# Three-part follow-up of a first product, and the order of two products around the masks, in an attention and mixture-of-experts kernel

## The chip, the cores and the metric

The kernel runs on one core of a Trainium2 chip. The metric is the device time of one execution in microseconds (us). The engines are PE (TensorE: matmuls; its weight loads are PEld), DVE (VectorE), ACT (ScalarE), POOL (GpSimd) and SP (SyncE, which only issues DMAs here). Each engine works through its own instructions in order; an instruction that waits holds back all that stands behind it on its engine.

## What is computed

Three networks follow each other: attention in which only scores within tau of the row's maximum count, a dense two-layer network with an ELU, and a layer of eight experts of which each token takes one.

```python
def _attn_ref(q, k, v, tau):                       # 2 batches, 8 heads, 576 tokens, 64 wide
    scores = scale * np.matmul(q, k.transpose(0, 1, 3, 2))
    thresh = np.max(scores, axis=-1, keepdims=True) - tau
    scores = np.where(scores >= thresh, scores, -1000000000.0)
    ...
    return np.matmul(attn, v)
def _moe_ref(x, w_in, w_out):                      # 1152 tokens, 512 -> 2048 -> 512
    h = x @ w_in
    g = np.where(h > 0.0, h, alpha * (np.exp(np.minimum(h, 0.0)) - 1.0))
    return g @ w_out
def _moe2_ref(x, w_gate, w1, w2, capacity):        # 8 experts, 512 -> 1024 -> 512
    expert_idx = np.argmax(x @ w_gate, axis=1)
    ...
    h = np.maximum(np.einsum('ecd,edf->ecf', disp, w1), 0.0)
    y = np.einsum('ecf,efd->ecd', h, w2)
```

## The kernel before

Matmuls run in float16 on numbers split in a high and a low half, with three products for one (high by high, high by low, low by high), so nearly every tile is followed by a copy of its high half (ACT) and a subtraction for its low half (POOL or DVE).

The 1152 tokens are nine tiles of 128. The first 38 passes of the program are **steps** (the loop over `i`, written out under a manual schedule, so that the order of the code is the order on every engine). Step `i` treats one pair of heads of one tile (four steps to a tile) and carries along pieces of the later networks:

- `emit_pv(i - 2)`: the product of the probabilities of two steps ago (`pt`) with the values (`vst`), into `pv`.
- `emit_max`: DVE takes the maxima of the two score tiles `s` (L267), and from them `nb` (L268) and `th` (L269). `emit_exp`: ACT's exponentials (L273) into `pp`. `emit_mask`: DVE's masks (L279), which also read `s`. A score tile has two buffers, so the scores of the next step (`emit_s`, L245) wait for the mask: those of the next step's first head stand behind the first mask, those of the second head are written at the end of the step.
- `emit_split` and `emit_pt`: ACT and POOL (L288, L289) split `pp` into `phl`, and a transposing DMA brings it into `pt` (L294).
- `conv_next`: in steps 0 to 16, the conversion of one of 32 chunks of the dense network's weights (three DVE, two ACT, one POOL instruction each).
- `emit_x`: after a tile's last pair, its attention output is normalized and transposed into `xt`.
- `piece()`: one **first product** (`mm1_chunk`, L386: 48 matmuls into the bank `mma`) or one **second product** (`mm2_chunk`, L416: 12 matmuls into the bank `mmb`) of the dense network, taken in turn where both are ready. A table, `FILL`, says how many a step gets: one ahead of the masks, the rest behind them. What follows a first product (`after`: ACT's `ef` L400 and L401, DVE's `gf` L402, ACT's `g` L405, POOL's `g` L406) is written by `flush`, at the end of the step or just ahead of the step's next first product, which needs the bank `mma` back.
- `settle` and `slot`, at the end of the step: when a tile's second products are complete, `route` writes the token rows `x` (`x2_hi` L440, `x2_lo` L445; two row buffers), transposes them (`x2t`), and over the next steps computes the logits (L513), chooses the expert and counts (`choose`), ranks and scatters the rows to memory (`place`, `dispatch`, an indirect DMA of POOL's queue, L494). Each call of `slot` moves every open route on to its next `yield`.
- `prep_k`, `prep_v`, `prep_q`: keys, values and queries are split ahead of use; the low half of a tile's queries is POOL's (L105, once in four steps).

After the steps a **tail** finishes the dense network (a while loop of single pieces, now ordered by the scheduler, and the last tile by `last_block`), and then the **experts** run (L664, L720) while their weights stream in (`stg`, `we`, L624, L627).

## Time and profile before

| what | value |
|---|---|
| time, median of 3 runs | 705.2 us (705.11 to 707.5) |
| time of the profiled execution | 703.61 us |
| its span, first to last instruction | 701.8 us |
| PE busy | 477.0 us (68%) |
| DVE, ACT, POOL busy | 387.8 (55%), 357.6 (51%), 267.7 us (38%) |
| mean granted clock of TensorE | 0.895 of full speed |

The profiled execution is 1.8 us longer than its span (what lies around the instructions) and 1.6 us shorter than the median. Busy shares are means over stages of different kinds; the rows below take them stage by stage. Times in rows are us from the start of the span.

### The profile page before, as it was taken

Reading aid. Unit: us, or ns where it says so; the run is one execution under the profiler, and the core shown is the slowest. Engines: PE = TensorE matmul, PEld = TensorE weight load, DVE = VectorE, ACT = ScalarE, POOL = GpSimd, SP = SyncE. Lnnn points to the kernel's source line nnn. Section 1 sums busy time; section 2 is a strip of 40 time slices with the busy share of each in tenths; the row PEclk is TensorE's granted clock in tenths of the full one; section 3 lists DMA queues with packets and bytes.
Section 4 is the critical chain, followed back from the end, with each engine's and each line's share of the span. In section 5 each row is a group of like instructions: output and inputs, shape, how many; then the busy total and the mean of one; then the engine's idle time right before and its main releaser. Section 6 shows DMA issues by size and latency. Waiting matters only on the chain. (4 is left out here: it accounts for less than half of the span.)

```text
span 701.8 us, 12999 instructions
## 1 busy us (share of the span) xinstructions
PE 477.0 (68%) x5343; PEld 382.2 (54%) x5343; DVE 387.8 (55%) x768; ACT 357.6 (51%) x511; POOL 267.7 (38%) x193
## 2 busy tenths in 40 slices
PE   1133455558455677587776778789778999887793
PEld 0022244346235445455554547556678999876781
DVE  1778895944962644453445543543862556664731
ACT  1455474654553544444355544444663776565641
POOL 1244563543451323234344433432233334153332
PEclk9999998878667799988899989999899999999897
DMA  6447576672764551822428453255764889888631
GB/s 217 118 126 191 156 189 186 140 187 39 175 163 121 140 128 35 222 65 50 113 54 226 87 94 59 58 98 152 263 230 98 248 239 253 259 247 255 201 88 48
DMA packets 150771, 105.59 MB, mean 150 GB/s; under 512 B 135209, under 2 KB 135209, under 8 KB 146608
## 3 DMA queue, kind: packets, MB, share of 16 engines
q1 hardware_dynamic: 148064, 99.94, 54.9%
q0 software_dynamic: 2640, 4.74, 1.9%
q8 instruction: 44, 0.72, 0.4%
q14 instruction: 23, 0.19, 0.1%
HBM read 60.06 MB, written 12.68 MB: 104 GB/s over the span
## 5 line engine op out<-in xcount | busy, mean ns | idle before, releaser
L386 PE MATMUL mma<-xt,wi 128*128 128x128 f16 x1728 | 119.1, 237 | 24.4 <-DVE gf L402 19.8
L386 PEld LDWEIGHTS <-wi 128*128 128x128 f16 x1728 | 115.4, 108 | 29.0 <-issue 21.6
L245 PE MATMUL s<-kst,qst 128*128 128x288 f16 (+1 forms) x320 | 58.4, 344 | 104.2 <-DVE pp L279 95.2
L289 POOL TENSOR_TENSOR phl<-pp,phl 128x1152 f16<-128x1152 f32 x36 | 85.3, 2370 | 102.9 <-issue 95.5
L416 PE MATMUL mmb<-wo,g 128*128 128x512 f16 x384 | 107.0, 439 | 17.5 <-DVE x L445 14.6
L402 DVE SCALAR_TENSOR_TENSOR gf<-ef,mma 128x512 f32<-128x512 f32 x36 | 24.7, 687 | 143.4 <-ACT ef L401 143.4
L245 PEld LDWEIGHTS <-qst 128*128 128x128 f16 (+1 forms) x320 | 30.1, 115 | 124.4 <-DVE pp L279 73.2
L627 DVE SCALAR_TENSOR_TENSOR we<-stg,we 128x1024 f16<-128x1024 f32 x64 | 79.0, 1268 | 32.3 <-ACT we L624 30.7
L273 ACT ACTIVATE pp<-s,nb,escale 128x576 f32<-128x576 f32 x72 | 55.9, 827 | 77.6 <-DVE nb L268 77.6
L624 ACT ACTIVATE we<-stg 128x1024 f16<-128x1024 f32 x64 | 64.3, 1048 | 43.6 <-DMA stg<-in_w_dram 42.8
L406 POOL TENSOR_TENSOR g<-gf,g 128x512 f16<-128x512 f32 x36 | 42.4, 1179 | 106.3 <-ACT g L405 106.2
L664 PE MATMUL mm<-xs,we 128*128 128x196 f16 x768 | 72.4, 259 | 14.8 <-DVE yt L731 5.2
L416 PEld LDWEIGHTS <-g 128*128 128x128 f16 x384 | 40.9, 111 | 71.2 <-issue 43.6
L664 PEld LDWEIGHTS <-we 128*128 128x128 f16 x768 | 69.1, 103 | 16.9 <-DVE we L627 9.1
L311 PE MATMUL pv<-vst,pt 128*128 128x64 f16 (+3 forms) x1080 | 52.9, 216 | 30.1 <-ACT vst L107 11.4
L311 PEld LDWEIGHTS <-pt 128*128 128x128 f16 (+1 forms) x1080 | 49.7, 114 | 37.3 <-issue 34.8
L677 POOL TENSOR_TENSOR ht<-rf,ht 128x392 f16<-128x392 f32 x32 | 35.6, 1123 | 77.7 <-issue 39.1
L279 DVE SCALAR_TENSOR_TENSOR pp<-s,th,pp 128x576 f32<-128x576 f32 x72 | 55.9, 814 | 15.2 <-ACT pp L273 15.2
L720 PE MATMUL mm<-ht,we 128*128 128x196 f16 x672 | 57.9, 247 | 1.7 <-DVE yt L731 1.7
L720 PEld LDWEIGHTS <-we 128*128 128x128 f16 x672 | 56.9, 97 | 1.8 <-issue 1.8
L400 ACT ACTIVATE ef<-mma 128x512 f32<-128x512 f32 x36 | 21.5, 596 | 71.3 <-PE mma L386 71.2
L288 ACT ACTIVATE phl<-pp 128x1152 f16<-128x1152 f32 x36 | 42.0, 1165 | 24.6 <-DVE pp L279 24.6
(123 smaller groups left out, 608.4 us busy)
## 6 DMA issues: line engine op xcount, KB each, us to landing
stg<-in_w_dram SPq DMA_DIRECT2D x32, 1024.0 KB, 6.1
cst<-in_w_in_dram SPq DMA_DIRECT2D x16, 512.0 KB, 4.5
cst<-in_w_out_dram SPq DMA_DIRECT2D x16, 512.0 KB, 4.0
disp<-zero SPq DMA_DIRECT2D x6, 771.0 KB, 4.7
qraw<-in_qt_dram SPq DMA_DIRECT2D x9, 512.0 KB, 3.4
vraw<-in_vb_dram SPq DMA_DIRECT2D x8, 320.0 KB, 5.9
kraw<-in_kt_dram SPq DMA_DIRECT2D x8, 288.0 KB
out_dram<-zero SPq DMA_DIRECT2D x1, 2304.0 KB
```

Of the source, the lines that this page charges most:

```text
L245: nc.tensor.matmul(s[a:z, half, 0:288], q2[:, pas, h, a:z], kst[b, h // 2][:, h % 2, half * 288:(half + 1) * 288], start=(pas == 0), stop= ...
L273: nc.scalar.activation(out=pp[:, z].rearrange("p (a c) -> p a c", a=2), in_=s, func=ACTF.Exp, bias=nb[:, z:z + 1], scale=escale,)
L279: nc.vector.scalar_tensor_tensor(out=e, in0=s, scalar=th[:, z:z + 1], in1=e, op0=ALU.is_ge, op1=ALU.mult, accum_out=rsum[t_][:, h:h + 1],)
L289: nc.gpsimd.tensor_tensor(out=d[:, 1], in0=flat, in1=d[:, 0], op=ALU.subtract)
L311: nc.tensor.matmul(o[a:e, h:h + w // D, :].rearrange("p h d -> p (h d)"), q[:, ph * 9 + blk, a:e], vt[:, vh, c:c + w], start=(blk == 4 and ...
L386: nc.tensor.matmul(ps[:, o * P:(o + 1) * P], w[:, wh, kk, :], xt[t_][:, xh * 4 + kk, :], start=(k_ == 0), stop=(k_ == 11),)
L406: nc.gpsimd.tensor_tensor(out=lo, in0=g, in1=hi, op=ALU.subtract)
L416: nc.tensor.matmul(ps, gt[t_, q][:, gh, o, :], w[:, wh, :], start=(first and o == 0 and n == 0), stop=(last_ and o == QF - 1 and n == 2),)
L624: nc.scalar.activation(out=w[:, 0, part], in_=t[:, part], func=ACTF.Copy, scale=SC)
L627: nc.vector.scalar_tensor_tensor(out=w[:, 1, part], in0=t[:, part], scalar=SC, in1=w[:, 0, part], op0=ALU.mult, op1=ALU.subtract)
L664: nc.tensor.matmul(ps[:, o * n:(o + 1) * n], w[:, wh, kk % 2, f * P:(f + 1) * P], t[:, xh * 4 + kk, :], start=(k_ == 0), stop=(k_ == 11),)
L720: nc.tensor.matmul(ps[:, o * n:(o + 1) * n], w[:, wh, f % 4, j * P:(j + 1) * P], h2[:, gh, f, :], start=(f == 0 and n_ == 0), stop=(f == 7 ...
```

## The change

Four things change. The generator `after` now yields twice, so that its five instructions come in three parts: ACT's two for `ef`; DVE's `gf`; the two halves of `g`. `flush(1)` moves every open one on by one part, and in a step it stands at three places: ahead of the maxima, behind the exponentials, and behind the first conversion, so a first product's follow-up goes into the **next** step. The pieces are ordered: ahead of the masks only second products (`piece(2)`; a first one only in a step with conversions, none open and no second product ready), and one first product, if one is ready, at the end of the step, just ahead of the second head's scores (`piece(1)`). `settle` and `slot` move ahead of that last piece. The matmuls of `choose` that count tokens become `count`, one `yield` later, so a route takes one slot more. `FILL` starts a step earlier.

```diff
-    FILL = [0] * 8 + [3] * 11 + [2] * (NTILE * NPAIR + LAG - 19)
+    FILL = [0] * 7 + [3] * 11 + [2] * (NTILE * NPAIR + LAG - 18)
...
             nc.scalar.activation(out=e, in_=e, func=ACTF.Exp, scale=-1.0, bias=lnsc)
+            yield
             nc.vector.scalar_tensor_tensor(
                 out=g, in0=e, scalar=-GS, in1=ps, op0=ALU.add, op1=ALU.max
             )
+            yield
             nc.scalar.activation(out=hi, in_=g, func=ACTF.Copy)
             nc.gpsimd.tensor_tensor(out=lo, in0=g, in1=hi, op=ALU.subtract)
-        return after
+        return after()
...
-        rk, oh, pr, slot_f = choose(rp)
+        oh, pr, slot_f = choose(rp)
+        yield
+        rk = count(rp[:, 64:64 + E], oh)
         yield
...
-    def flush():
-        while evac:
-            evac.pop(0)()
-
-    def piece():
+    def flush(stages=3):
+
+        for _ in range(stages):
+            for g in list(evac):
+                if next(g, g) is g:
+                    evac.remove(g)
+
+    def piece(first=0):
         a, b = pick1(), pick2()
         if a is None and b is None:
             return False
-        if b is None or (a is not None and turn[0] == 0):
+        if first == 2 and b is None:
+            return False
+        if b is None or (a is not None and first < 2):
...
-            g_at[a, q] = step[0]
+            g_at[a, q] = step[0] + 1
...
+            flush(1)
             if on:
                 lim = emit_max([sc[z] for z in range(2)])
                 for z in range(2):
                     emit_exp(sc[z], lim[0], pair_p[i], z)
+            flush(1)
             if nc_:
                 conv_next()
-            if nf:
-                piece()
+            flush(1)
+            for _ in range(nf - 1):
+                piece(2) or (nc_ and not evac and piece(1))
             if on:
...
                 emit_split(i)
                 emit_pt(i)
+            settle()
...
-            for _ in range(nf - 1):
-                piece()
+            slot()
+            if nf:
+                piece(1)
             if i + 1 < NSTEP:
                 sc[1] = emit_s((i + 1) // NPAIR, (2 * i + 3) % H)
-            flush()
-            settle()
...
-            slot()
...
-        piece()
+        piece(1 + step[0] % 2)
```

What the planner makes of it: the steps from 7 to 18 hold 11 first products instead of 12 (two each in steps 7, 11, 12 and 15, one in 16, 17 and 18; before, two in 8, three in 11, one in 12, three in 15, one in 17, two in 18). From step 19 on every step has one second and one first product in both kernels. The tail gets one first product more.

DVE in a step in which a tile's output `xf` is normalized and a route chooses its expert (rows mx to slot_f). Before, from the masks (L279) to the next step's maxima:

```order
L279 SCALAR_TENSOR_TENSOR pp,rsum<-s,th,pp 128x576 x2
L324 TENSOR_SCALAR rinv<-rsum 128x8
L325 RECIPROCAL rinv<-rinv 128x8
L327 TENSOR_TENSOR xf<-pv,rinv 128x512
L402 SCALAR_TENSOR_TENSOR gf<-ef,mma 128x512
L453 TENSOR_REDUCE mx<-mmc 128x1
L454 SCALAR_TENSOR_TENSOR cand<-mmc,mx,ev 128x8
L457 TENSOR_REDUCE amin<-cand 128x1
L459 TENSOR_SCALAR oh<-ev,amin 128x8
L463 TENSOR_SCALAR nmx<-mx 128x1
L467 TENSOR_SCALAR slot_f<-amin 128x1
L267 TENSOR_REDUCE m<-s 128x1 x2
```

Now, the same kind of step from its own maxima on:

```order
L267 TENSOR_REDUCE m<-s 128x1 x2
L268 TENSOR_SCALAR nb<-m,cmul 128x2
L269 TENSOR_SCALAR th<-m,cadd 128x2
L403 SCALAR_TENSOR_TENSOR gf<-ef,mma 128x512
L279 SCALAR_TENSOR_TENSOR pp,rsum<-s,th,pp 128x576 x2
L324 TENSOR_SCALAR rinv<-rsum 128x8
L325 RECIPROCAL rinv<-rinv 128x8
L327 TENSOR_TENSOR xf<-pv,rinv 128x512
L455 TENSOR_REDUCE mx<-mmc 128x1
```

`gf`, which waits for the first product, stood between the masks and the next maxima; now it stands between a step's own maxima and its masks.

ACT in a step that also prepares the queries (qraw, qst) and writes rows (x). Before, from the exponentials (L273) on:

```order
L273 ACTIVATE pp<-s,nb,escale 128x576 x2
L288 ACTIVATE phl<-pp 128x1152
L400 ACTIVATE ef<-mma 128x512
L401 ACTIVATE ef<-ef,lnsc 128x512
L405 ACTIVATE g<-gf 128x512
L103 ACTIVATE qraw<-qraw 128x1024
L104 ACTIVATE qst<-qraw 128x1024
L440 ACTIVATE x_3727<-mmb 128x512
```

Now:

```order
L273 ACTIVATE pp<-s,nb,escale 128x576 x2
L407 ACTIVATE g<-gf 128x512
L288 ACTIVATE phl<-pp 128x1152
L464 ACTIVATE pr<-mmc,nmx 128x8
L442 ACTIVATE x_3584<-mmb 128x512
L103 ACTIVATE qraw<-qraw 128x1024
L104 ACTIVATE qst<-qraw 128x1024
L400 ACTIVATE ef<-mma 128x512
L401 ACTIVATE ef<-ef,lnsc 128x512
L273 ACTIVATE pp<-s,nb,escale 128x576 x2
```

The rows `x` come ahead of the queries, and the two `ef` instructions now stand behind the queries, directly ahead of the next exponentials.

DVE in step 22, where the third tile's rows are written (x_3007; the first tile's rows, x_2159, hold one of the two row buffers). Now, from the scatter's numbers on:

```order
L490 CAST slot_i<-slot_f 128x1
L491 TENSOR_REDUCE den<-pr 128x1
L492 TENSOR_SCALAR den<-den 128x1
L493 RECIPROCAL den<-den 128x1
L495 TENSOR_SCALAR x_2159<-den 128x1
L496 COPY x_2159<-ids 128x1
L497 TENSOR_TENSOR cum<-cum,oh 128x8
L447 SCALAR_TENSOR_TENSOR x_3007<-mmb,x_3007 128x512
L267 TENSOR_REDUCE m<-s 128x1 x2
```

Before, a whole step lay between the first tile's `cum` row and the third tile's rows; now the rows follow in the same step.

## Rows read from the trace of the kernel before

**Rows 1.** Four stretches: busy us of each engine (instructions), granted clock, DMA share, GB/s.

```profile
95.00:275.00 180.00, 107.79 (x1189) 81.86 (x1190) 110.78 (x189) 94.51 (x133) 78.63 (x53) 0.80 0.55 137
275.00:463.00 188.00, 139.82 (x1640) 101.38 (x1638) 86.55 (x249) 87.48 (x117) 72.38 (x44) 0.88 0.45 100
463.00:536.00 73.00, 62.84 (x803) 49.76 (x802) 39.15 (x109) 38.77 (x60) 22.17 (x17) 0.92 0.62 186
536.00:673.00 137.00, 120.58 (x1353) 118.24 (x1352) 78.56 (x98) 85.94 (x131) 51.31 (x41) 0.96 0.80 228
```

**Rows 2.** Line L268, two stretches: count, ns min/median/max, first and last start in us.

```profile
L268 DVE TENSOR_SCALAR nb<-m,cmul x13: 228/297/557, 95.2 to 274.9; 128x2 f32<-128x2 f32 x13
...
L268 DVE TENSOR_SCALAR nb<-m,cmul x17: 228/228/554, 274.9 to 462.9; 128x2 f32<-128x2 f32 x17
```

**Rows 3.** Waits from 275 to 463: who for whom, us in total, times, longest.

```profile
DVE gf L402 <- ACT ef L401: 77.2, 16, 6.7
...
PE mmb L416 <- DVE x L445: 14.6, 4, 4.8
```

**Rows 4.** Timeline, step 28: start, us, engine, line, op, tiles [idle before <-releaser].

```profile
384.01 1.15 POOL L406 TENSOR_TENSOR g<-gf,g 128x512 f16<-128x512 f32 x1 [2.60 <-ACT g L405]
384.64 0.55 DVE L268 TENSOR_SCALAR nb<-m,cmul 128x2 f32<-128x2 f32 x1
...
387.04 0.66 PE L245 MATMUL s<-kst,qst 128*128 128x288 f16 x4 [1.99 <-DVE pp L279]
...
387.54 2.84 PE L386 MATMUL mma<-xt,wi 128*128 128x128 f16 x48
...
390.22 0.65 PE L245 MATMUL s<-kst,qst 128*128 128x288 f16 x4
...
391.01 1.03 PE L311 MATMUL pv<-vst,pt 128*128 128x128 f16 x27
...
391.45 2.68 SPq L294 DMA_TRANSPOSE pt<-phl  x1
...
391.87 0.69 DVE L402 SCALAR_TENSOR_TENSOR gf<-ef,mma 128x512 f32<-128x512 f32 x1 [4.15 <-ACT ef L401]
391.88 2.75 PE L416 MATMUL mmb<-wo,g 128*128 128x512 f16 x12
392.47 1.42 DVE L267 TENSOR_REDUCE m<-s 128x1 f32<-128x576 f32 x2
```

**Rows 5.** Timeline, step 30, with queries and rows; columns as in rows 4.

```profile
408.26 2.38 POOL L289 TENSOR_TENSOR phl<-pp,phl 128x1152 f16<-128x1152 f32 x1 [4.46 <-issue]
...
412.79 0.69 DVE L402 SCALAR_TENSOR_TENSOR gf<-ef,mma 128x512 f32<-128x512 f32 x1 [5.87 <-ACT ef L401]
...
415.12 1.06 ACT L104 ACTIVATE qst<-qraw 128x1024 f16<-128x1024 f32 x1
416.08 0.58 ACT L440 ACTIVATE x<-mmb 128x512 f16<-128x512 f32 x1
416.26 2.13 POOL L105 TENSOR_TENSOR qst<-qraw,qst 128x1024 f16<-128x1024 f32 x1 [0.88 <-ACT qst L104]
...
417.44 4.44 PE L416 MATMUL mmb<-wo,g 128*128 128x512 f16 x12 [4.84 <-DVE x L445]
```

**Rows 6.** Timeline, step 11 (conversions and three first products); columns as in rows 4.

```profile
149.87 5.23 PE L386 MATMUL mma<-xt,wi 128*128 128x128 f16 x48 [5.14 <-DVE gf L402]
...
157.27 4.33 PE L386 MATMUL mma<-xt,wi 128*128 128x128 f16 x48 [2.16 <-DVE gf L402]
...
163.08 0.69 DVE L402 SCALAR_TENSOR_TENSOR gf<-ef,mma 128x512 f32<-128x512 f32 x1 [5.86 <-ACT ef L401]
...
165.13 0.55 DVE L268 TENSOR_SCALAR nb<-m,cmul 128x2 f32<-128x2 f32 x1
```

**Rows 7.** DMA issues: tiles, queue, count, median us from issue to landing.

```profile
pt<-phl SPq DMA_TRANSPOSE x36, 4.6
...
disp<-x,slot_i POOLq DMA_INDIRECT x9, 3.2
```

More of the change, by code (lines that the diff above doesn't have):

```diff
@@ L447, in x2_lo, with choose @@
         )
-    def choose(rp, rk=None):
+    def choose(rp):
         lg = rp[:, 0:E]
@@ L459, in choose @@
         nc.vector.tensor_scalar(oh, ev, amin, None, ALU.is_equal)
-        rk = (rp if rk is None else rk)[:, 64:64 + E]
-        nc.tensor.matmul(rk, ones, cum, start=True, stop=False, skip_group_check=True)
-        nc.tensor.matmul(rk, tri, oh, start=False, stop=True, skip_group_check=True)
         nc.vector.tensor_scalar(nmx, mx, -I2, None, ALU.mult)
@@ L467, in choose, with count @@
         nc.vector.tensor_scalar(slot_f, amin, float(CS), float(E * CS), ALU.mult, ALU.add)
-        return rk, oh, pr, slot_f
+        return oh, pr, slot_f
+    def count(rk, oh):
+        nc.tensor.matmul(rk, ones, cum, start=True, stop=False, skip_group_check=True)
+        nc.tensor.matmul(rk, tri, oh, start=False, stop=True, skip_group_check=True)
+        return rk
     def rank(rk, oh):
@@ L576, in route_last @@
         x2 = row.bitcast(F16)
-        rk, oh, pr, slot_f = choose(rp, mm_bank())
+        oh, pr, slot_f = choose(rp)
+        rk = count(mm_bank()[:, 64:64 + E], oh)
         bank = []
@@ L779 @@
     evac = []
-    turn = [0]
     def ready(kind, q, ahead=0):
@@ L824, in piece @@
             return False
-        if b is None or (a is not None and turn[0] == 0):
+        if first == 2 and b is None:
+            return False
+        if b is None or (a is not None and first < 2):
             q = nq1[a]
             nq1[a] += 1
-            turn[0] = 1
             bank = "a"
@@ L831, in piece @@
             evac.append(mm1_chunk(a, q, bank))
-            g_at[a, q] = step[0]
+            g_at[a, q] = step[0] + 1
             return True
         t_, q1 = b
-        turn[0] = 0
         if not summing:
```

## Prediction

> **What bounds the kernel now.** I read the stretches first, then the waits, then the order of events in single steps. The stretches [rows 1] show four stages. The experts (536 to 673) keep PE busy 120.6 of 137 us; the change does not touch them. The tail (463 to 536) has PE busy 62.8 of 73 us. The two stretches of steps are different: from 95 to 275 no engine is busy much over 60% of 180 us, and from 275 to 463 PE is busy 139.8 of 188 us at a granted clock of 0.88, DVE and ACT less than half. So the steps wait rather than work. The waits [rows 3] name it: DVE stood 77.2 us in 16 steps in front of `gf`, for ACT's `ef`, and PE 14.6 us in four steps in front of a second product, for DVE's `x2_lo`.
>
> One undisturbed step shows the loop [rows 4]. Between `nb` at 384.64 and the end of the next maxima at 393.89, where the next `nb` starts, lie 9.25 us, and each link waits for the one before it: nb to the first head's scores 2.40 (exponential, mask), to the first product 0.50, to the second head's scores 2.68, to `gf` 1.65 (ACT's two `ef` instructions), to the next maxima 0.60, their length 1.42. The scores were written by 390.87, but the maxima start at 392.47, because `gf` stands ahead of them on DVE and waits for the first product's follow-up. The end of step 30 shows what else stands there [rows 5]: from `gf` at 412.79 DVE dispatches rows and waits for ACT's queries and rows, and PE stands 4.84 us until 417.44, then works its second product at the lower clock (4.44 us instead of 2.75). Sixteen steps from step 19 to step 35 take 274.9 to 462.9, 188.0 us or 11.75 each [rows 2].
>
> In the earlier stretch the same follow-up is paid once for every first product that another one follows: in step 11 the second starts at 149.87 and the third at 157.27 [rows 6], 7.40 us apart, each having waited for `gf` of the one before; and behind the third, from `gf` at 163.08 to `nb` at 165.13, 2.05 us, with the two `ef` ahead of it.
>
> **Steps 19 to 34.** What the change removes from the loop is `gf` with its wait, and everything that `settle` and `slot` put between `gf` and the maxima. What is left of the serial chain, from the start of the second head's scores: the scores 0.65, the second maximum 0.71 (half of 1.42), some 0.15 of hand-over, then nb to the first head's scores 2.40: 3.9 us. PE meanwhile has 390.22 to 391.01 (scores, logits in this step), `pv` 0.87 and a second product 2.75: 4.1 us without the logits. So PE is late last, by a little. A step is then PE's own work: scores and first product 0.50 + 2.68, scores 0.49, `pv` 0.87, second product 2.75, together 7.3 us [rows 4], all at full clock, which I take since PE would hardly idle and the experts, with PE busy 88%, are granted 0.96 [rows 1].
>
> The rest is moved, not removed. `ef` runs while the second head's scores and maxima do. `gf` stands between `th` and the masks, where DVE waits for the exponential anyway; if `ef` is late, the masks are late by as much. `hi` of `g` stands ahead of `phl` on ACT, which waits for the second mask; `lo` of `g` (1.15 on POOL) ends about when POOL's `phl` can start. `x2_lo` and `dispatch` run beside PE's first product (2.68) and scores. The probabilities: the transposing DMA was issued 6.81 us after `nb` (391.45) and lands 4.6 later [rows 7], 11.4 in all; `pv` asks for it two steps on, two steps of 7.3 less the 1.5 by which `nb` follows the scores, 13.1 us, plus 0.5. The cover is thin (about 2 us) but holds.
>
> Three costs are added.
>
> First, the queries. In one step of four ACT's two passes and then POOL's 2.13 us [rows 5] now fall on the next step's `nb`. What happens then, rows 4 show: `nb` took 0.55 us at 384.64 where its median is 0.228 [rows 2], and ended at 385.19, with POOL's instruction of 384.01 to 385.16. DVE's small instruction does not finish while POOL's runs. Count from the start of the second head's scores: `nb` follows about 1.5 later (scores, second maximum, hand-over), the probabilities' DMA 6.8 behind that, at 8.3; POOL's 2.38 for `phl` [rows 5] comes before it, so ACT's split ends at about 5.8. Then follow ACT's rows, 0.58, and two passes of 1.06 each, to 8.5, and POOL's queries, to 10.6, while the next `nb` is due at 7.3 + 1.5 = 8.8 and takes 0.23: 1.6 us late, of which PE's margin takes 0.2, so 1.4. A fourth kind of step has `dispatch` run into POOL's `phl` in the same way; I take 0.7. With the logits (0.45), that is 2.6 us in four steps, 0.65 a step. I round 7.95 up to 8.0.
>
> The Trainium skill ("SBUF — State Buffer", section "Who interferes with whom") has this as a lock: of a DVE instruction in a two-port mode and a GpSimd one, whichever starts first holds the shared ports for its whole length and the other blocks fully. The trace agrees in the 0.55 above. It speaks against the change: with the lock a step is 8.0, without it 7.5, and the total 8 us less.
>
> Second, the row buffer. In step 22 the third tile's rows need the buffer that the first tile's scatter, issued in the same step, still reads, since a route now takes a slot more. The scatter stands on POOL behind `phl`, so it starts about 8.3 us after the scores began and lands 3.2 later [rows 7], 11.5; then ACT's rows 0.58, DVE's as long as its `gf`, 0.69, and the next maxima 1.42: 14.2 instead of 8.8, over 5 us, and PE idles meanwhile and comes back at the lower clock, some 1.5 more: 6.5 us, once. For the later tiles the scatter lies at least a step ahead.
>
> Third, 1.5 us for loads and zero fills that now share fewer microseconds with the probabilities.
>
> Sum: 16 x 8.0 + 6.5 + 1.5 = 136 against 188: **-52 us**. Bounds: PE's bare 7.3 a step without any of the small collisions (117 + 6.5, -64 us); and the loop of rows 4 as it is, 9.25, without what `slot` adds to it (148 + 6.5, -33 us). I choose nearer the first, because each link of the shorter chain has its row, and keep both for the range.
>
> **Steps 7 to 18** take 95.2 to 274.9, 179.7 us [rows 2]. Steps 11 and 15 lose a third first product each, 7.40 [rows 6]: -14.8. Six steps ended in a first product (8, 11, 12, 15, 17, 18) and no longer have its follow-up between the scores and the maxima: 6 x 2.15 (the 2.05 of rows 6, and a little for `ef`): -12.9. Step 18 has one first product for two: its 2.84 [rows 4] and a wait for `gf` of about half a microsecond, -3.4. Step 12 gets a second one behind a first: 7.40, less the second product of 2.75 that leaves it: +4.6. The second products that go to steps 13 and 14, and the one first product of step 16, run beside conversions. Sum **-26.5 us**; bounds -18 (step 12 pays in full, and loads of keys and values hold steps 15 to 18) and -34 (PE's clock stays up in those steps; the 4.33 and 5.23 of rows 6 were at the lower one).
>
> **Tail.** One first product more, 2.84 [rows 4], and routes that end a slot later: **+3.5 us**; between 0 (it fills PE's 10 idle us of 73 [rows 1]) and 7.4 (it stands alone with its follow-up, as in rows 6). The steps 0 to 6 and the experts stay.
>
> **Total.** -52 - 26.5 + 3.5 = -75 us. From the profiled execution's own 703.6 us that gives 628.6; the median of the runs is 1.6 us above the profiled one, so against 705.2 it would be 630. I say **628 us**. The ends of the three parts give 606 (-64, -34, 0) and 660 (-33, -18, +7.4).
>
> **Rivals.**
>
> *Another engine closes the loop (0.17).* DVE and ACT have long in-order queues; if `ef` comes late behind the queries, the masks, the scores and PE follow, and a step is 9 to 10 us rather than 8. For it: ACT's 87.5 us in 16 steps is 5.5 a step, with three hand-overs to DVE in each. Against it: nothing on ACT between the masks and the first product's end fills more than 5 us except in the query step. Time: 16 x 1 to 2 us more, 645 to 660.
>
> *Row buffer or probabilities late at every tile (0.07).* If not only step 22 waits for its scatter but each of six later tiles, or `pv` for its DMA as often, at 6.5 us each it is 39 us more: 667. For it: two buffers, a route of six slots, a new tile every four steps, and only about 2 us of cover for `pv`. Against it: after step 22 the scatter comes at least a step before the rows that need its buffer.
>
> *The clock (0.03), the other side.* If denser work on PE brought the granted clock down to its lower level, a step would be 14.6 us instead of 7.3, sixteen of them 234, and the whole 703.6 + 46 - 26.5 + 3.5 = 727 us, slower than before. It decides from a mean clock of about 0.55 in the steps: there, 16 x 7.3 / 0.55 = 212 us eat up both gains. For it: the steps from 95 to 275 had 0.80 [rows 1]. Against it: that stretch had PE busy 60%, the experts with 88% had 0.96, and the slow second product of rows 5 came behind 4.84 us of idling.
>
> *The gain does not come (0.03).* Some order that I misread keeps the old loop, and only the third first products are saved: about 688.
>
> **Numbers.** The forecast's own case, 605 to 645 us, holds 0.70, the rivals 0.17, 0.07, 0.03 and 0.03. For 8 in 10 I take 606 to 656: the forecast's case and most of the first rival. Half a per cent is about what a measurement of this kernel can tell from no change: faster by more 0.95, within it 0.02, slower by more 0.03.
>
> **What would show it.** In the changed kernel's profile the starts of `nb` in steps 19 to 35 should lie 7.3 to 9 us apart, except behind step 22 (about 14). DVE's wait for `ef` should fall from 77 to under 15 us, PE's wait for `x2_lo` should be gone but for step 22, and PE's clock in these steps should be above 0.93. Steps 11 and 15, with two first products each, should take about 16 us. `nb` behind the queries should be long. The forecast is wrong if steps stand at 9 us or more with PE waiting for DVE's masks, if `pv` waits for its DMA, if ACT's rows wait for the scatter at more than one tile, or if the tail grows by over 8 us.

## The result: 634 us, 0.897 of the time before

Timed beside the kernel before on one chip, the changed kernel took 634.18 us (median of 4 runs, 631.46 to 635.73) against 706.35 us (4 runs, 705.11 to 709.11): a ratio of 0.897, 95% interval 0.892 to 0.902. A second set on another occasion gave 632.22 us (6 runs) against 704.73 (11 runs): 0.896, 0.893 to 0.899. The prediction was 628 us, 606 to 656. The profiled execution took 635.48 us, its span is 633.7, and the mean granted clock 0.925 instead of 0.895.

Steps 19 to 34 of the changed kernel (columns as in rows 1):

```profile
253.00:390.00 137.00, 123.37 (x1639) 92.15 (x1638) 101.57 (x238) 85.01 (x117) 72.29 (x44) 0.96 0.68 134
```

PE is busy 123 of 137 us; before, it was busy 140 of 188 [rows 1]. It executes the same matmuls, faster, at a clock of 0.96 instead of 0.88. The starts of `nb` bound the steps (count, shortest, median and longest ns, first and last start):

```profile
L268 DVE TENSOR_SCALAR nb<-m,cmul x12: 228/230/927, 96.2 to 244.1; 128x2 f32<-128x2 f32 x12
...
L268 DVE TENSOR_SCALAR nb<-m,cmul x16: 228/228/2178, 253.2 to 383.5; 128x2 f32<-128x2 f32 x16
```

Steps 7 to 18 take 253.2 - 96.2 = 157 us (179.7 before), and steps 19 to 34, up to the next `nb` at 390.3, 137.1 us (188.0 before) [rows 2], 8.6 each instead of 11.75.

The waits of that stretch, in the form of rows 3. A line for DVE's `gf` waiting for ACT's `ef`, 77.2 us before [rows 3], is not among them any more:

```profile
ACT ef L400 <- PE mma L386: 17.7, 12, 2.7
DVE x L447 <- ACT x L442: 13.4, 4, 6.6
DVE m L267 <- PE s L245: 11.6, 10, 2.5
...
ACT x L442 <- DMA disp<-x,slot_i: 8.5, 1, 8.5
...
PE mmb L418 <- DVE x L447: 6.5, 1, 6.5
...
PE pv L311 <- DMA pt<-phl: 3.0, 2, 2.5
...
PE s L245 <- DVE pp L279: 2.3, 5, 1.1
```

DVE and ACT now wait for PE (the first and third lines). The ten waits of the maxima lie in nine of the 16 steps. In the other seven (19, 20, 22, 28, 29, 31 and 33) the maxima follow other work of DVE without a wait, as in step 28 (timeline):

```profile
337.93 2.37 POOL L289 TENSOR_TENSOR phl<-pp,phl 128x1152 f16<-128x1152 f32 x1 [0.45 <-POOL g L408]
338.31 2.01 DVE L497 TENSOR_TENSOR cum<-cum,oh 128x8 f16<-128x8 f16 x1
...
340.24 1.41 DVE L267 TENSOR_REDUCE m<-s 128x1 f32<-128x576 f32 x2
```

`cum` starts without a wait and lasts until POOL's `phl` ends, and the maxima come right behind it. PE waits once for rows, 6.5 us, behind the one wait for the scatter, and hardly for the masks.

Step 24, undisturbed, from its `nb` to the next (timeline; what is in brackets is idle time before, and who ended it):

```profile
301.89 0.23 DVE L268 TENSOR_SCALAR nb<-m,cmul 128x2 f32<-128x2 f32 x1
...
302.16 0.68 DVE L403 SCALAR_TENSOR_TENSOR gf<-ef,mma 128x512 f32<-128x512 f32 x1
...
304.36 0.65 PE L245 MATMUL s<-kst,qst 128*128 128x288 f16 x4
...
304.90 2.84 PE L386 MATMUL mma<-xt,wi 128*128 128x128 f16 x48
...
307.58 0.65 PE L245 MATMUL s<-kst,qst 128*128 128x288 f16 x4
...
308.27 0.76 DVE L267 TENSOR_REDUCE m<-s 128x1 f32<-128x576 f32 x1 [2.46 <-PE s L245]
...
308.93 2.75 PE L418 MATMUL mmb<-wo,g 128*128 128x512 f16 x12
309.06 0.23 DVE L268 TENSOR_SCALAR nb<-m,cmul 128x2 f32<-128x2 f32 x1
```

From 301.89 to 309.06 are 7.17 us, and no PE instruction in it has an idle time in front. `gf` follows `nb` without a wait, and the second maximum waits 2.46 us for the scores where it used to wait for `gf` [rows 4].

Step 22, the long one:

```profile
277.55 0.65 DVE L268 TENSOR_SCALAR nb<-m,cmul 128x2 f32<-128x2 f32 x1
...
282.05 2.38 POOL L289 TENSOR_TENSOR phl<-pp,phl 128x1152 f16<-128x1152 f32 x1 [0.45 <-POOL g L408]
...
282.43 2.02 DVE L497 TENSOR_TENSOR cum<-cum,oh 128x8 f16<-128x8 f16 x1
...
284.60 1.15 POOL L498 DMA_INDIRECT disp<-x,slot_i  x1 [0.17 <-PE s L245]
...
290.44 0.60 ACT L442 ACTIVATE x<-mmb 128x512 f16<-128x512 f32 x1 [8.52 <-DMA disp<-x,slot_i]
...
291.81 5.00 PE L418 MATMUL mmb<-wo,g 128*128 128x512 f16 x12 [6.45 <-DVE x L447]
...
293.12 2.18 DVE L268 TENSOR_SCALAR nb<-m,cmul 128x2 f32<-128x2 f32 x1
293.16 2.12 POOL L105 TENSOR_TENSOR qst<-qraw,qst 128x1024 f16<-128x1024 f32 x1 [7.41 <-ACT qst L104]
```

ACT's rows wait 8.52 us for the scatter, DVE's rows and the maxima stand behind them, PE idles 6.45 us and returns at the lower clock (5.00 instead of 2.75). The step takes 15.58 us. In the last two lines, and in `cum` beside `phl`, a DVE instruction of a few elements lasts until POOL's ends.

Where the 68.1 us went (us, from the starts of `nb` in the profiled executions; the last two columns are the time of that execution and the median):

| kernel | to step 0 | steps 0-6 | steps 7-18 | steps 19-34 | behind | profiled | median |
|---|---|---|---|---|---|---|---|
| before | 23.1 | 72.1 | 179.7 | 188.0 | 238.9 | 703.61 | 706.35 |
| changed | 24.1 | 72.1 | 157.0 | 137.1 | 243.4 | 635.48 | 634.18 |
| changed, again | 25.0 | 72.1 | 157.6 | 134.8 | 243.3 | 634.86 | 632.22 |
| follow-up whole | 23.2 | 72.1 | 172.9 | 184.7 | 243.7 | 698.18 | 696.68 |
| settle late | 23.7 | 72.1 | 163.6 | 135.0 | 244.9 | 641.22 | 638.29 |
| pieces as before | 24.8 | 72.1 | 162.4 | 138.2 | 235.9 | 635.06 | 636.25 |
| count early | 23.3 | 72.1 | 158.7 | 145.5 | 239.5 | 641.51 | 639.94 |
| queries on DVE | 23.8 | 77.1 | 160.7 | 136.2 | 244.3 | 643.98 | 642.74 |
| three rows | 25.3 | 72.1 | 156.7 | 127.2 | 246.5 | 629.69 | 628.83 |
| short second product | 24.9 | 72.1 | 156.4 | 138.9 | 246.1 | 640.28 | 634.59 |
| zeros in parts | 23.7 | 72.1 | 157.2 | 134.8 | 239.5 | 629.25 | 631.65 |
| rows and zeros | 25.0 | 72.1 | 158.4 | 128.8 | 239.5 | 625.92 | 626.53 |

The column "behind" holds the tail and the experts, up to the end of the span. The first expert matmul parts them, before and now:

```profile
L664 PE MATMUL mm<-xs,we x768: 244/248/373, 535.9 to 672.3; 128*128 128x196 f16 x192
...
L671 PE MATMUL mm<-xs,we x768: 244/248/373, 470.7 to 604.9; 128*128 128x196 f16 x192
```

The tail grew from 73.0 to 80.5 us, and what follows it fell from 165.9 to 162.9.

The two executions of the changed kernel show how far a column can be trusted: 1 us in steps 7 to 18, 2 in steps 19 to 34.

### The profile page after: what moved, and what is told of

It is laid out like the page before. It is cut to its first block, busy times and chain, and to the rows that moved or that the text cites. A ratio compares the mean times of both kernels' runs of the same rounds, so it can differ in the third digit from the quotient of the medians.

```text
span 633.7 us, 13023 instructions
## 1 busy us (share of the span) xinstructions
PE 452.4 (71%) x5343; PEld 367.6 (58%) x5343; DVE 405.0 (64%) x768; ACT 354.4 (56%) x511; POOL 267.8 (42%) x193
## 4 chain that ended last, share of the span: by engine, by line
DVE 38%; DMA 22%; PE 16%; ACT 11%; issue 10%; POOL 2%; SPq 1%; DVEq 0%; POOLq 0%; ACTq 0%
DMA stg<-in_w_dram 8%; PE mma L386 8%; DVE pp L279 7%; DVE m L267 6%; DMA out_dram<-y,ix 5%; DVE cvp L359 4%; DVE we L634 3%; DVE cvp L358 3%; PE mmb L418 3%; DMA pt<-phl 3%; DMA yr<-yt 2%; DVE kst L213 2%; PE s L245 2%; ACT we L631 2%; DVE cvp L362 2%
## 5 line engine op out<-in xcount | busy, mean ns | idle before, releaser
L386 PE MATMUL mma<-xt,wi 128*128 128x128 f16 x1728 | 116.2, 233 | 33.1 <-DVE gf L403 33.1
L386 PEld LDWEIGHTS <-wi 128*128 128x128 f16 x1728 | 111.2, 106 | 37.1 <-issue 25.4
L245 PE MATMUL s<-kst,qst 128*128 128x288 f16 (+1 forms) x320 | 56.2, 333 | 72.5 <-DVE pp L279 63.4
L418 PE MATMUL mmb<-wo,g 128*128 128x512 f16 x384 | 95.8, 403 | 12.1 <-DVE x L447 6.5
L289 POOL TENSOR_TENSOR phl<-pp,phl 128x1152 f16<-128x1152 f32 x36 | 85.3, 2371 | 14.8 <-POOL g L408 9.2
L273 ACT ACTIVATE pp<-s,nb,escale 128x576 f32<-128x576 f32 x72 | 55.9, 827 | 49.2 <-DVE nb L268 49.1
L671 PE MATMUL mm<-xs,we 128*128 128x196 f16 x768 | 69.6, 253 | 14.3 <-DVE g L754 4.8
L671 PEld LDWEIGHTS <-we 128*128 128x128 f16 x768 | 66.7, 100 | 16.2 <-DVE we L634 8.1
L418 PEld LDWEIGHTS <-g 128*128 128x128 f16 x384 | 37.5, 103 | 56.7 <-issue 22.3
L311 PE MATMUL pv<-vst,pt 128*128 128x64 f16 (+3 forms) x1080 | 48.5, 208 | 30.7 <-DVE xf L327 11.9
L267 DVE TENSOR_REDUCE m<-s 128x1 f32<-128x576 f32 x72 | 52.0, 750 | 27.0 <-PE s L245 26.7
L311 PEld LDWEIGHTS <-pt 128*128 128x128 f16 (+1 forms) x1080 | 46.2, 108 | 37.1 <-issue 30.5
L727 PEld LDWEIGHTS <-we 128*128 128x128 f16 x672 | 57.4, 98 | 2.4 <-issue 2.3
L279 DVE SCALAR_TENSOR_TENSOR pp<-s,th,pp 128x576 f32<-128x576 f32 x72 | 55.9, 813 | 4.4 <-ACT pp L273 4.3
L288 ACT ACTIVATE phl<-pp 128x1152 f16<-128x1152 f32 x36 | 41.9, 1165 | 12.7 <-DVE pp L279 12.7
```

Source lines behind the costliest of these rows:

```text
L245: nc.tensor.matmul(s[a:z, half, 0:288], q2[:, pas, h, a:z], kst[b, h // 2][:, h % 2, half * 288:(half + 1) * 288], start=(pas == 0), stop= ...
L267: nc.vector.tensor_reduce(out=m[:, z:z + 1], in_=sc[z], axis=AX.XY, op=ALU.max)
L273: nc.scalar.activation(out=pp[:, z].rearrange("p (a c) -> p a c", a=2), in_=s, func=ACTF.Exp, bias=nb[:, z:z + 1], scale=escale,)
L279: nc.vector.scalar_tensor_tensor(out=e, in0=s, scalar=th[:, z:z + 1], in1=e, op0=ALU.is_ge, op1=ALU.mult, accum_out=rsum[t_][:, h:h + 1],)
L289: nc.gpsimd.tensor_tensor(out=d[:, 1], in0=flat, in1=d[:, 0], op=ALU.subtract)
L311: nc.tensor.matmul(o[a:e, h:h + w // D, :].rearrange("p h d -> p (h d)"), q[:, ph * 9 + blk, a:e], vt[:, vh, c:c + w], start=(blk == 4 and ...
```

## Experiments

**Which part of the change carries the gain.** Three kernels undo one part each.

The follow-up whole again, at the end of the step:

```diff
-            flush(1)
...
-            flush(1)
...
-            flush(1)
...
                 sc[1] = emit_s((i + 1) // NPAIR, (2 * i + 3) % H)
+            flush()
```

> The changed kernel with the follow-up of a first product written whole at the end of the step, as before the change; the order of the pieces, the earlier settle and slot and the later count stay. My theory, that the three parts in the next step take gf out of the way of the maxima and that this is the larger part of the gain: the steps 19 to 34 take 9.2 to 9.7 us each instead of 8.6, and up to 160 us together instead of 137; the steps from 7 to 18 lose some 10 us as well; the time is 660 to 672. DVE's wait for ef comes back (over 40 us in these steps). Rival, that the gain comes from settle and slot, which no longer stand between gf and the maxima: within 5 us of 634.

Measured: 696.68 us, 0.989 of before (0.984 to 0.995). Nearly all of the gain is gone, more than I had expected. Its step 27 (timeline):

```profile
364.93 0.56 DVE L268 TENSOR_SCALAR nb<-m,cmul 128x2 f32<-128x2 f32 x1
...
368.05 0.28 PE L245 MATMUL s<-kst,qst 128*128 128x288 f16 x1 [2.78 <-DVE pp L279]
...
373.28 0.69 DVE L403 SCALAR_TENSOR_TENSOR gf<-ef,mma 128x512 f32<-128x512 f32 x1 [4.63 <-ACT ef L401]
373.88 1.42 DVE L267 TENSOR_REDUCE m<-s 128x1 f32<-128x576 f32 x2
```

The scores of 371.63 are written by 372.28, but the maxima begin at 373.88, behind `gf`: the loop of rows 4 again, 10.4 us here, with PE waiting 2.78 us for the mask in it. The second product is ahead of the masks and `settle` and `slot` are early in this kernel, so neither of them opens the loop by itself. The kernel undoes two things at once, the parts and their move into the next step; a follow-up written whole at the start of the next step was not run.

`settle` and `slot` back at the step's end:

```diff
-            settle()
...
-            slot()
             if nf:
                 piece(1)
...
+            settle()
...
+            slot()
```

> The changed kernel with settle and slot back at the end of the step, behind the last first product and the scores; the three parts and the order of the pieces stay. My theory, that their place hardly matters once gf is out of the way, since DVE and ACT come to them at the same time as before (only PE's logits and counting matmuls move, and ACT's queries go ahead of the rows): 632 to 638 us. Rival, that moving them ahead of the last piece is a main part of the gain: 650 us or more, with PE waiting for x2_lo ahead of second products again.

Measured: 638.29 us, 0.905 (0.900 to 0.910). Steps 19 to 34 take 135.0 us, as in the changed kernel; the loss is in steps 7 to 18 (163.6 against 157.0 and 157.6). So what `settle` and `slot` put ahead of the maxima costs nothing in steps 19 to 34 once `gf` is out of the way.

The pieces in their old order and number, the follow-up in three parts:

```diff
-    FILL = [0] * 7 + [3] * 11 + [2] * (NTILE * NPAIR + LAG - 18)
+    FILL = [0] * 8 + [3] * 11 + [2] * (NTILE * NPAIR + LAG - 19)
...
-            for _ in range(nf - 1):
-                piece(2) or (nc_ and not evac and piece(1))
+            if nf:
+                piece()
...
-            if nf:
-                piece(1)
+            for _ in range(nf - 1):
+                piece()
```

> The changed kernel with the pieces in turn and in the table of before (up to three first products in a step of the conversions); the three parts, the earlier settle and slot and the later count stay. My theory, that the order of the pieces matters in steps 7 to 18 alone, where a first product behind another waits for gf behind the conversions: these steps take 168 to 176 us instead of 157, the steps from 19 on about the same 137, the tail 3 to 4 us less; the time is 642 to 650. Rival, that the three parts make up for it since a first product's follow-up now starts the next step: within 4 us of 634.

Measured: 636.25 us, 0.904 (0.899 to 0.909), nearer to the rival. The order gains 5 us in steps 7 to 18 (162.4 against 157.0 and 157.6) and gives them back behind the steps (235.9 against 243.4), where the changed kernel has one first product more. From step 19 on the two orders come to the same, 138.2.

**Three places where the change makes things collide or moves them apart.**

A third row buffer (its space comes from a third `acc`):

```diff
-            x2acc[t_] = shared.tile([P, DM], F32, name="acc", tag="acc", bufs=3)
+            x2acc[t_] = shared.tile([P, DM], F32, name="acc", tag="acc", bufs=2)
...
-        row = shared.tile([P, ROW], U16, name="x2", tag="x2", bufs=2)
+        row = shared.tile([P, ROW], U16, name="x2", tag="x2", bufs=3)
...
```

> The changed kernel with three buffers for the token rows instead of two (the accumulator of the second products gives up one of its three, which the plan never needs). My theory, that step 22 is long because ACT's write of the third tile's rows waits for the first tile's scatter: step 22 falls from 15.6 us to 8 to 9, ACT no longer waits 8.5 us for the indirect DMA, and the time falls by 6 to 8 us to about 627 (ratio to the kernel before 0.886 to 0.890). Rival, that step 22 is long because of the zero fills and loads in those steps, which delay the probabilities: step 22 stays above 13 us and the time within 2 us of 634.

Measured: 628.83 us, 0.893 (0.889 to 0.896). Step 22 of this kernel (timeline):

```profile
282.75 0.58 ACT L442 ACTIVATE x<-mmb 128x512 f16<-128x512 f32 x1
...
285.29 0.68 DVE L447 SCALAR_TENSOR_TENSOR x<-mmb,x 128x512 f16<-128x512 f32 x1
285.53 1.15 POOL L498 DMA_INDIRECT disp<-x,slot_i  x1 [0.17 <-PE s L245]
...
286.12 2.75 PE L418 MATMUL mmb<-wo,g 128*128 128x512 f16 x12
```

ACT writes the rows 2.78 us before the scatter is even issued, and the second product runs at full clock. Step 22 falls from 15.58 to 8.86 us: 6.7 us, for which the prediction had 6.5. Steps 19 to 34 are 7.6 to 9.9 us shorter than in the two executions of the changed kernel, but 3 us come back behind the steps (246.5 against 243.4), and the medians differ by 3 to 5 us; the intervals of the two ratios overlap.

The query's low half on DVE instead of POOL:

```diff
-            nc.gpsimd.tensor_tensor(out=lo, in0=src, in1=hi, op=ALU.subtract)
+            nc.vector.tensor_tensor(out=lo, in0=src, in1=hi, op=ALU.subtract)
```

> The changed kernel with the low half of a tile's queries subtracted on DVE instead of POOL (tiles 1 to 8, once in four steps), everything else as it is. My theory, that nb is held up in these steps by POOL's instruction and not by ACT's queue: the long nb (1.75 us at 325.5, 2.18 at 293.1) goes back to 0.23, the steps behind the queries lose 1 to 1.5 us each, DVE gets 1.2 us more at the end of seven steps where it waits for the scores, and the time falls by 4 to 9 us to 625 to 630. Rival, that these steps are late because ef comes late on ACT: within 2 us of 634, the masks starting as late as now. A third way: the DVE instruction itself is held up by POOL's phl and comes into the way of the maxima, slower by 3 to 8 us.

Measured: 642.74 us, 0.911 (0.906 to 0.916): slower than the changed kernel, where I had expected 625 to 630. What it moves, first in the changed kernel, at the start of step 27:

```profile
325.05 2.13 POOL L105 TENSOR_TENSOR qst<-qraw,qst 128x1024 f16<-128x1024 f32 x1 [0.24 <-ACT qst L104]
...
325.46 1.75 DVE L268 TENSOR_SCALAR nb<-m,cmul 128x2 f32<-128x2 f32 x1
...
329.15 0.65 PE L245 MATMUL s<-kst,qst 128*128 128x288 f16 x4 [1.06 <-DVE pp L279]
```

`nb` lasts until POOL's instruction ends, 1.75 us for 0.23, and PE waits 1.06 us; step 27 takes 8.38 us, 1.2 more than step 24. With the low half on DVE the same place reads:

```profile
333.86 1.23 DVE L105 TENSOR_TENSOR qst<-qraw,qst 128x1024 f16<-128x1024 f32 x1 [1.34 <-ACT qst L104]
...
335.00 1.42 DVE L267 TENSOR_REDUCE m<-s 128x1 f32<-128x576 f32 x2
...
336.45 0.23 DVE L268 TENSOR_SCALAR nb<-m,cmul 128x2 f32<-128x2 f32 x1
```

`nb` is short again, and step 27 falls from 8.38 to 6.87 us. But DVE now stands 1.34 us in front of its new instruction, for ACT's queries, with both maxima behind it, and step 26 rises from 7.12 to 9.25. In steps 6 and 10, where ACT's queries come later, the loss is larger (step 10: 7.64 to 12.05). So the lock is real and its price was right, but the lock is the cheaper of the two: POOL's wait for ACT holds up nothing, DVE's holds up the maxima.

The counting matmuls back with the choice:

```diff
         oh, pr, slot_f = choose(rp)
-        yield
         rk = count(rp[:, 64:64 + E], oh)
```

> The changed kernel with the counting matmuls back in choose, so that a route takes one slot less. My theory: two effects. PE now stands in front of the counting matmuls, ahead of the step's first product, until DVE has chosen the expert, 1.5 to 2 us in each of about seven routes, +8 to +12 us; and step 22 no longer waits for the scatter, -6.5. Together 636 to 640. Rival, that PE's wait is hidden because the masks are late anyway: only the second effect is left, 627.

Measured: 639.94 us, 0.909 (0.903 to 0.914). Steps 25, 29 and 33 take 12.7 to 13.75 us, since PE, its first product behind the count, waits for the choice (3.76 us in step 25); step 22, in turn, falls to 8.37, with routes a slot shorter. The extra slot is worth more than the row buffer that it costs.

**Is PE really the bound?** Second products of 8 matmuls instead of 12 (the high half of `g` by the low half of the weights is left out):

```diff
-            for n, (gh, wh) in enumerate(((0, 0), (0, 1), (1, 0))):
+            for n, (gh, wh) in enumerate(((0, 0), (1, 0))):
...
```

> The changed kernel with the second products cut to two thirds: the product of the high half of g with the low half of the weights is left out (8 matmuls instead of 12 a piece, except in the last tile), so PE has 0.87 us less in each step that holds one. My theory, that PE is late last in a step but by little: DVE's chain (scores, maxima, exponential, mask) closes the loop after 0.2 to 0.4 us, so the steps from 19 to 34 lose 3 to 6 us together, and the tail and the other steps up to 6: 622 to 630. Rival, that PE alone bounds these steps: 14 us less in them, and 612 to 617 in all. Other rival, that another engine bounds them already: nothing in them, 630.

Measured: 634.59 us, 0.900 (0.895 to 0.904): no gain, though PE is busy 114.7 us in steps 19 to 34 instead of 123.5. That is the other rival, and not the 3 to 6 us that I expected. In seven steps (19, 20, 28, 29, 32, 33 and 34) the period is that of the changed kernel to 0.01 us, so PE's work did not set it there. In steps 21, 24 and 26 it falls, by 0.2 to 0.4 us. In steps 23, 25 and 27 it rises, by 1.2 to 2.0 us; step 23 (timeline):

```profile
291.96 3.57 PE L418 MATMUL mmb<-wo,g 128*128 128x512 f16 x8 [6.42 <-DVE x L447]
...
297.39 1.12 PE L245 MATMUL s<-kst,qst 128*128 128x288 f16 x4 [1.85 <-DVE pp L279]
...
298.30 4.28 PE L386 MATMUL mma<-xt,wi 128*128 128x128 f16 x48
```

PE waits 1.85 us for the mask, and what follows runs at the lower clock: the scores take 1.12 instead of 0.65, the first product 4.28 instead of 2.84, the step 10.6 us instead of 8.8. It was not this wait that brought the clock down: the second product of step 22, behind 6.42 us of idling, ran at the lower clock already, as it did in the changed kernel. There the same scores waited 0.43 us, and they and the first product ran at full clock; the granted clock of step 23 is 0.62 here and 0.81 there. Where nothing is late (step 24), the shorter product takes the period from 7.17 to 6.78 only, and the mask closes the loop (PE waits for it in all 16 steps, 14.8 us in total, against 5 steps and 2.3 us above). So in such a step PE and the chain over DVE and ACT are 0.4 us apart. The profiled execution of this kernel took 5.7 us more than its median, so the size of the loss at the lower clock is uncertain; that the median gained nothing is not.

**The zero fill.** In step 27 of the changed kernel one DMA of 2.3 MB (written at the end of step 26) fills the output with zeros. The issues of the probabilities' next two DMAs last 5.5 and 5.0 us, where 2.7 is usual, and two steps on `pv` waits for them:

```profile
333.46 5.53 SPq L294 DMA_TRANSPOSE pt<-phl  x1
...
340.33 5.03 SPq L294 DMA_TRANSPOSE pt<-phl  x1
...
350.69 1.53 PE L311 MATMUL pv<-vst,pt 128*128 128x128 f16 x27 [2.55 <-DMA pt<-phl]
```

In nine parts, one a step:

```diff
...
-            if i == ZOUT:
-                zero_out()
+            if ZOUT <= i < ZOUT + NTILE:
+                zero_out(i - ZOUT)
```

> The changed kernel with the zeros of the output written in nine parts, one a step from step 26 on, instead of 2.3 MB in step 26. My theory, that this DMA makes the probabilities late behind it (pv waits 2.5 us at 350.7, the probabilities' DMA of step 28 took 10.8 us to issue with the next, and steps 29 and 30 are long): step 30 falls from 10.9 to about 8, the time by 2 to 4 us to about 631. Rival, that the probabilities are late for another reason: within 1 us of 634.

Measured: 631.65 us, 0.897 (0.892 to 0.902), the ratio of the changed kernel itself. `pv` waits no longer, and step 30 falls from 10.85 to 6.78 us, but the median does not show the 4 us. Step 31 rises from 7.98 to 9.53, since its `nb` now starts beside POOL's queries and lasts 1.91 us, where in the changed kernel it took 0.36:

```profile
356.16 2.13 POOL L105 TENSOR_TENSOR qst<-qraw,qst 128x1024 f16<-128x1024 f32 x1
...
356.40 1.91 DVE L268 TENSOR_SCALAR nb<-m,cmul 128x2 f32<-128x2 f32 x1
```

The changed kernel was run once more, beside the next kernel:

> The changed kernel itself once more, timed beside the next kernel on the same chip, so that the two differ by their edits alone. Expected 629 to 636 us, 0.892 to 0.902 of the kernel before.

Measured: 632.22 us, 0.896 (0.893 to 0.899). In this execution of the same program the two `pv` behind the zero fill read:

```profile
342.68 1.04 PE L311 MATMUL pv<-vst,pt 128*128 128x128 f16 x27 [0.40 <-DMA pt<-phl]
...
351.30 1.04 PE L311 MATMUL pv<-vst,pt 128*128 128x128 f16 x27 [1.34 <-DMA pt<-phl]
```

The wait is there, but 1.34 us of it did not bring the clock down (2.55 did: `pv` 1.53, the second product 3.93), and step 30 takes 7.98 us. Steps 30 and 31 together take 16.31 us here, and 16.31 with the zeros in parts; in the first execution they took 18.83. So 2.5 of the 10.85 us belong to one execution, and the rest of what the zeros in parts take out of step 30 comes back in step 31.

> Third row buffer and zero fill in nine parts together. My theory: step 22 falls from 15.6 to about 8.9 us and step 30 from 10.9 to about 7, so 8 to 10 us less in steps 19 to 34 (127 to 129 us), of which the work behind the steps gives back 0 to 4, as it did with the third row buffer alone: 5 to 9 us faster than the changed kernel on the same chip, 624 to 629 us. Rival: both edits move the same few microseconds (step 30 falls with the row buffer alone), and the experts wait for their weights anyway: within 3 us of the third row buffer alone, 628 to 631 us.

Measured (third row buffer and zeros in parts): 626.53 us (623.56 to 628.72, 6 runs), 0.889 (0.885 to 0.892), the fastest of all and 5.7 us under the changed kernel on the same chip. Step 22 takes 8.86 us and step 30 6.79, as expected, but step 31 takes 9.53: steps 30 and 31 together are 16.32 us, as with the third row buffer alone, so there the rival was right. Behind the steps it takes 239.5 us against 243.3 (246.5 with the row buffer alone); why, no run here tells, and the ratios of the two kernels with three rows are not clear of each other's noise. In its step 25 PE waits 1.71 us for the logits' bank, as in the changed kernel, and this time the first product behind it runs at the lower clock:

```profile
308.90 0.44 PE L517 MATMUL mmc<-wg,x2t 128*128 128x8 f16 x12 [1.71 <-DVE rj L476]
...
309.20 4.47 PE L386 MATMUL mma<-xt,wi 128*128 128x128 f16 x48
```

The step takes 10.91 us there, 9.29 in the changed kernel.

## Why the prediction was right, and where it was off

The prediction's sum against its own profiled execution was -75 us, measured -68.1: -50.9 in steps 19 to 34 (predicted -52), -22.7 in steps 7 to 18 (-26.5), +4.5 behind the steps (+3.5), and +1.0 ahead of step 0 (nothing; it varies from 23.1 to 25.3 between kernels). The third of these agrees by luck: the tail alone grew by 7.5 us, just past the prediction's upper end of 7.4, and the experts and the end, which were to stay, took 3.0 less.

*The loop.* Shown right in what it removes. With the follow-up in three parts the wait for `ef` is gone, and in a step without other work PE's own work sets the period: 7.17 us in step 24, predicted 7.3. With the follow-up whole the loop is back and with it 47.6 of the 50.9 us, whatever the order of the pieces. That `settle` and `slot` were part of what the change takes out of the loop was a wrong share of it: put back at the step's end they cost steps 19 to 34 nothing. I read the end of step 30 [rows 5], where rows and queries stand behind `gf`, as an added cost; with `gf` out of the way they fit beside PE's work.

*The choice between PE and the chain.* Predicted 4.1 against 3.9 us, PE later by a little; the shortened product shows 0.4 us between them in step 24. But the prediction took this choice for every step, and in at least seven of the 16 PE's work did not set the period. In five of those (19, 20, 28, 29 and 33) DVE comes to the maxima late from other work. The 0.7 us for `dispatch` was right (step 28: 7.84 against 7.17), but two kinds of step had no term: steps 19 and 20 (8.93 and 8.51), where the conversion of the values (`vst`, 2.53 and 2.37 us) stands ahead of the maxima and PE has more to do for `pv` as well, and steps 29 and 33 (7.96 and 7.97), where the choice of the expert does. That the 14 steps without 22 and 30 still take 7.9 us each, for the predicted 8.0, is luck in part: these four are 4.7 us over step 24 together, and the other ten came out below their price.

*The collisions.* The lock of `nb` by POOL: predicted 1.4 us in the query step, measured 1.2 in step 27 (and moving the work off POOL costs more). The Trainium skill ("SBUF — State Buffer", section "Who interferes with whom") also says that a DVE instruction with two SBUF inputs contends with a GpSimd instruction that reads SBUF; `cum`, with two inputs of 128x8, agrees: 2.02 us beside `phl`, 0.31 in the median. The row buffer: predicted 6.5 us, measured 6.7 by taking it away. Its parts were off, though: the scatter was issued as predicted (8.5 us after the scores, predicted 8.3), but its rows came free 5.8 us later where I had taken 3.2 [rows 7]; the DMA table of the changed kernel has

```profile
disp<-x,slot_i POOLq DMA_INDIRECT x9, 5.7
```

The 1.5 us that I put down for the lower clock, in turn, were not paid: the slow second product ended at 296.81, and the next scores, at 297.24, were waiting for the mask, which was late behind the held `nb`. So a total that was right holds two errors that cancel, by luck.

*What was not priced.* PE's wait in front of the logits in step 25 (1.71 us, for `rj`, which stands behind the tile's normalization on DVE), and the zero fill ahead of the probabilities, which I had put with other loads at 1.5 us in all and which cost `pv` 3.0 us of waiting (and steps 30 and 31 2.5 us in one execution, where the clock fell, nothing in the other).

*Steps 7 to 18.* The mis-sized term. Steps 11 and 15 fell by 16.1 us (8.3 and 7.8), where the prediction had 14.8 for the third products and 4.3 for the follow-ups; steps 9 and 13, which had no term, rose by 2.6 together; step 18 fell by 9.3 instead of 5.6. A step with conversions still holds two first products one behind the other, and the second still waits, 5.14 us in step 11, for the first one's `gf`:

```profile
149.86 0.69 DVE L403 SCALAR_TENSOR_TENSOR gf<-ef,mma 128x512 f32<-128x512 f32 x1 [2.40 <-ACT ef L401]
...
150.60 5.28 PE L386 MATMUL mma<-xt,wi 128*128 128x128 f16 x48 [5.14 <-DVE gf L403]
```

Nor was the split right: by the experiment with the old order of the pieces the rest of the change brings 17.3 of the 22.7 us, where I had 12.9 for it, and the order 5.4, where I had 13.6 net for the products that it removes and moves. What lies behind the steps then takes back more than that (7.5 us between those two kernels): the tail is 71.0 us with the old order and 80.5 with the new one, where the prediction had 3.5 for it.

*The rivals.* Another engine closing the loop came true in part: not through a late `ef` and not at 9 to 10 us a step, but DVE's queue set the period of five steps, at 7.8 to 8.9 us. The scatter was late at one tile, as the forecast said, not at each; the clock rose (0.88 to 0.96) rather than fell. Of what the forecast asked to see, the wait of `gf` for `ef`, PE's wait for `x2_lo` outside step 22, the clock above 0.93 and the long `nb` behind queries came out. Two things did not: steps 11 and 15 took 17.1 and 18.3 us instead of about 16, and some steps lie outside 7.3 to 9 (step 25 at 9.29, step 30 at 10.85, five between 6.8 and 7.2), with step 22 at 15.58 instead of about 14. And one of the signs of being wrong came: `pv` waited for its DMA, twice, behind the zero fill; it cost 2.5 us at most.

## What to carry to other kernels

An instruction that waits for a long product belongs where its engine would wait anyway, not ahead of the next link of the serial loop; splitting one follow-up into parts by what each part waits for, and moving them into the next step, was worth 62 us here, and the order of what stands around it 2 to 6. When the loop has come down to little more than the work of one engine, look step by step at which engine ends it, and count again what a buffer must outlive and which small instructions now coincide with long ones on the neighbour: 6.7 us of one step lay in one more buffer, though about half of it came back later, and moving work off the engine that blocks was a loss, because the in-order queue that took it had the more urgent work behind it.

## What the runs showed of the hardware that was not expected

Less work on PE did not make the kernel faster. With second products a third shorter PE was busy 8.8 us less in steps 19 to 34, and the steps took 138.9 us instead of 134.8 to 137.1, at a granted clock of 0.93 instead of 0.96 and 0.97. Seven steps kept their period, and in steps 25 and 27, behind 2.08 and 2.30 us of idling, the first products ran at the lower of the two levels for the most part (4.04 and 3.99 us instead of 2.84). The same gap need not have the same effect twice: after 1.71 us of idling in step 25 the first product took 2.84 us in one kernel and 4.47 in another. What decides between the two these runs do not settle.

The scatter of the rows landed a median of 5.7 us after its issue in the changed kernel, 3.2 before [rows 7], for the same number of packets. Why, no run here tells.
